# A transformer block on one core: transposes of the identity where the plan leaves TensorE without a product

## The chip, the core and the metric

The kernel runs on one core of one Trainium2 chip. The metric is the device time of one execution in microseconds (us). The core's engines each follow their own list of instructions: TensorE (PE in the profile, its weight loads PEld), VectorE (DVE), ScalarE (ACT), GpSimd (POOL) and SyncE (SP), which issues most transfers. They meet only through semaphores that an instruction waits for or raises.

## The reference

The block takes one sequence of 2048 tokens of width 512. A conditioning vector gives six rows (shift, scale and gate, twice). First comes attention with 32 heads of width 16 on a modulated layer norm, then a "spatial shift" MLP block on another modulated layer norm:

```python
h = _layernorm(x) * (1 + ca) + sa
x = x + ga * _A_ref(h, A_wqkv, A_wo)            # softmax(q k / 4) v, then @ wo
h = _layernorm(x) * (1 + cb) + sb
x = x + gb * _B_ref(h, B_w1, B_w2, B_w3, B_w4)

def _B_ref(x, w1, w2, w3, w4):
    h = _gelu(_layernorm(x) @ w1)                # 512 -> 512
    # four quarters of the columns shifted by +1, -1, +2, -2 tokens
    x1 = x + concat(shifted quarters) @ w2
    return x1 + _gelu(_layernorm(x1) @ w3) @ w4  # 512 -> 1792 -> 512
```

All inputs and the output are float32.

## The kernel before

The 2048 tokens are cut into four chunks (`ci` 0 to 3) of four tiles of 128 tokens. Up to about 1490 us the kernel makes q, k and v and runs attention; then come the **tails**, one per chunk: `tail(ci)` (L1322) and `rest(ci)` (L1622). A tail transposes the attention output (tiles `xT<-ident,osb`), multiplies by wo (`wo`), adds to x, normalises twice (tiles `xf` or `xn`), transposes the result (`xT<-ident,xf` or `xT<-ident,xn`, L1283), and multiplies by w1, w2, w3 and w4 (all named `w` in the profile; `w<-A,wr` are w1 and w3, `w<-wr,g` are w2 and w4). Each product is made of three matmuls per step (`mm3`, lines L377, L379, L381), since every operand stands as a high and a low part. Chunk 0's tail is added while attention still runs; the tails of chunks 1 to 3 are added after it.

The order on each engine is fixed when the program is built. A small planner (`Sched`, from L103) keeps a planned time for each engine (`T["P"]` for TensorE) and a list of generators, each of which yields either planned nanoseconds of a product just issued or a condition that it waits for. `one()` runs the first generator that can go on. Work on ScalarE, VectorE and GpSimd is put in chains and issued by planned time. After attention the loop `while sch.busy(): sch.step()` (L1805) runs everything that is left. `step` (L304) moves TensorE's planned time on by 100 ns:

```python
        t = self.T["P"] + q                      # q = 100.0
        for e in "ADG":
            self.misc(e, max(t, self.T[e]) + 500)
        while self.T["P"] < t and self.one():
            pass
        self.T["P"] = max(self.T["P"], t)
```

Where `one()` finds no generator that can go on, planned time just passes. TensorE's list then has no mark of it; on the chip TensorE goes straight to its next matmul and waits there if its operands aren't ready.

A product's result goes to one of eight PSUM banks. `room()` (L285) says whether the plan has a free one, `dbank` takes it (`take`, L264, the first of `avail`), and the chain that reads it gives it back (`free`). The identity `ident` is a 128x128 float32 tile made at the start; a transpose is a matmul whose other operand it is.

Of the kernel before, what the change touches and what calls it, by code (L numbers as in the profile page):

```python
# [21 lines left out]
P = 128  # L22
# [92 lines left out]
class Sched:  # L115
# [4 lines left out]
    def __init__(self):  # L120
        self.pend = []
        self.chains = []
        self.gens = []
        self.credit = 0.0
        self.T = {"P": 0.0, "A": 0.0, "D": 0.0, "G": 0.0, "S": 1000.0}
        self.end = 0.0
        self.busyG = 0.0, 0.0
        self.gapmin = GAPMIN
        self.banks(8)
# [174 lines left out]
    def step(self, q=100.0):  # L304

        t = self.T["P"] + q
        for e in "ADG":
            self.misc(e, max(t, self.T[e]) + 500)
        while self.T["P"] < t and self.one():
            pass  # L310
        self.T["P"] = max(self.T["P"], t)


# [26 lines left out]
def kernel(ctx, tc, A_x, A_wqkv, A_wo, B_w1, B_w2, B_w3, B_w4, c, w_mod, out):  # L340
    nc = tc.nc
    te, act, dve, pool, dma = nc.tensor, nc.scalar, nc.vector, nc.gpsimd, nc.sync
# [62 lines left out]
    ident = con.tile([P, P], F32, name="ident")  # L405
# [33 lines left out]
    sch = Sched()  # L439
# [3 lines left out]
    def dbank(n):  # L443
        return sch.take(lambda i: psd["d"].tile([P, CH], F32, name=n, tag=f"s{i}" if psd["s"] else f"d{i}", bufs=1))
# [313 lines left out]
    for i in range(NV):  # L758
        t = qp.tile([P, H // 4, 192], BF16, name=f"vt{i}")
# [943 lines left out]
    for k, blk in enumerate(blocks + [[]] * (LAG + CPER)):  # L1703
# [19 lines left out]
        t, start = CIN, 0.0  # L1723
# [68 lines left out]
    with ExitStack() as ex:  # L1792
        ep = ex.enter_context(tc.tile_pool(name="ep", bufs=1, space=PSUM))
        psd["d"], psd["s"] = ep, False
        att.close()
        akx.close()
        tpx = ExitStack()
        tp = tpx.enter_context(tc.tile_pool(name="tp", bufs=1))
        big["A"] = tp.tile([P, 4 * KT * 2 * P], F32R, name="A")
        big["g2"] = tp.tile([P, 4 * KT * 2 * P], F32R, name="g2")  # L1800
        done.add("C")
        rings["f"] = Ring(FRONT * (NC - NB), [("wf", BF)] * BF)
        for ci in range(NB, NC):
            sch.add(tail(ci))
        while sch.busy():  # L1805
            sch.step()
        tpx.close()
# [29 lines left out]
```

## Time and profile before

| | |
|---|---|
| median of 3 runs | 1982.68 us (1981.67 to 1983.91) |
| the profiled execution's own time | 1985.08 us |
| its span, first to last instruction | 1983.3 us |
| TensorE busy | 1935.0 us (98%) |
| VectorE, ScalarE, GpSimd busy | 1535.5, 1497.2, 1546.2 us |
| mean granted TensorE clock | 0.991 |

"Span" is the time that the profile covers; the execution's own time is 1.8 us longer. A busy TensorE isn't one at its peak: matmuls overlap, so the time between two starts in a dense row is less than the time that each is shown with. The granted clock is the share of the full clock that TensorE was given in a stretch; in this trace it is either 1.00 or 0.50 at any moment, so a value between is a mixture. In the timeline a row has the start, the time, the engine, the line, what is written from what, and, in brackets, the idle time ahead of it and the instruction that ended it.

### The profile page before, as it was taken

How to read it: one execution, taken by the hardware profiler on the slowest of the kernel's cores; microseconds unless marked ns; L12 is line 12 of the kernel's file. 1: busy time of each engine (PE TensorE's matmuls, PEld its weight loads, DVE VectorE, ACT ScalarE, POOL GpSimd, SP SyncE). 2: the span in 40 equal slices, each digit the busy share in tenths (PEclk: the TensorE clock that was granted, in tenths of full speed). 3: DMA queues.
4: the chain of work that ended last, by engine and by line, in shares of the span. 5: the costliest groups of instructions: out<-in, count | busy, mean ns of one | idle time of the engine just before them, and what ended most of it. 6: DMA issues, size and time to landing. Idle time of an engine off the chain costs nothing.

```text
span 1983.3 us, 41283 instructions
## 1 busy us (share of the span) xinstructions
PE 1935.0 (98%) x14456; PEld 1158.8 (58%) x14456; DVE 1535.5 (77%) x2672; ACT 1497.2 (75%) x3067; POOL 1546.2 (78%) x1445
## 2 busy tenths in 40 slices
PE   8999999999999999999999999999998999999999
PEld 5745544555444444444444444444456889899998
DVE  6398788888899999999999999999975583423211
ACT  6448898777899999999999999999986454334222
POOL 6359998888899999999999999999995564335222
PEclk9999999999999999999999999999999899999999
DMA  8877656544535353435353535354513587554541
GB/s 303 234 218 182 158 139 169 146 125 126 128 73 109 74 109 74 105 77 108 74 106 77 101 81 106 77 143 124 108 50 144 211 297 283 201 196 152 202 149 69
DMA packets 185502, 277.95 MB, mean 140 GB/s; under 512 B 117104, under 2 KB 127856, under 8 KB 169008
## 3 DMA queue, kind: packets, MB, share of 16 engines
q1 hardware_dynamic: 181792, 267.20, 49.5%
q10 hardware_dynamic: 2304, 4.20, 0.7%
q0 software_dynamic: 1200, 3.93, 0.5%
q8 instruction: 114, 1.87, 0.4%
q14 instruction: 92, 0.75, 0.1%
HBM read 211.81 MB, written 62.91 MB: 139 GB/s over the span
## 4 chain that ended last, share of the span: by engine, by line
PE 77%; DVE 12%; ACT 6%; issue 2%; POOL 1%; DMA 1%; SPq 0%; ACTq 0%; DVEq 0%; POOLq 0%
PE mb L1021 17%; PE sc L1048 11%; PE pv L1122 11%; DVE mx L1017 10%; PE w L379 7%; PE w L381 7%; PE w L377 7%; PE pv L1119 5%; ACT pt L1044 3%; PE ot L1149 3%; PE xT L1283 1%; PE q L379 1%; PE q L377 1%; PE q L381 1%; PE v L377 1%
## 5 line engine op out<-in xcount | busy, mean ns | idle before, releaser
L1017 DVE TENSOR_REDUCE mx<-mb 128x1 f32<-128x512 f32 x2048 | 1251.9, 681 | 56.0 <-PE mb L1021 48.4
L1097 POOL TENSOR_SCALAR pt<-pt 128x1024 f16<-128x1024 uint16 x770 | 1015.2, 1368 | 62.7 <-ACT pt L1044 62.4
L1044 ACT ACTIVATE pt<-sc 128x512 int32<-128x512 f32 x1688 | 891.0, 621 | 89.1 <-PE mb L1021 61.1
L1021 PE MATMUL mb<-kst,qtl 62*128 62x512 f32 x2048 | 784.8, 462 | 18.0 <-ACT pt L1044 9.1
L1048 PE MATMUL sc<-qtl,kst 64*128 64x512 f32 x2048 | 745.2, 451 | 0.5 <-ACT pt L1044 0.4
L1021 PEld LDWEIGHTS mb<-kst,qtl 62*128 62x128 f32 x2048 | 360.3, 192 | 259.6 <-ACT pt L1044 131.9
L1048 PEld LDWEIGHTS sc<-qtl,kst 64*128 64x128 f32 x2048 | 337.8, 185 | 186.5 <-DVE mx L1017 114.9
L1122 PE MATMUL pv<-pt,vst 128*32 128x512 f16 x3376 | 319.0, 396 | 3.3 <-ACT ac L1139 3.3
L1536 POOL TENSOR_TENSOR g<-sq,g 128x256 fp32r<-128x256 f32 (+1 forms) x122 | 95.7, 786 | 179.8 <-ACT g L1535 168.1
L1097 POOL TENSOR_SCALAR xbs<-xbs 128x1024 f16<-128x1024 uint16 x163 | 216.9, 1362 | 3.8 <-ACT xbs L1044 3.7
L1044 ACT ACTIVATE xbs<-sc 128x512 int32<-128x512 f32 x360 | 199.5, 639 | 11.2 <-PE mb L1021 10.1
L1122 PEld LDWEIGHTS <-vst 128*32 128x32 bf16 x4096 | 91.2, 94 | 181.0 <-issue 163.5
L1533 ACT ACTIVATE sq<-w 128x256 f32<-128x256 f32 (+1 forms) x128 | 52.0, 406 | 183.2 <-PE w L381 182.8
L1655 DVE TENSOR_TENSOR x<-x,w 128x512 f32<-128x512 f32 x73 | 49.7, 684 | 168.8 <-PE w L381 168.7
L1119 PE MATMUL pv<-pt,vst 128*32 128x512 f16 (+1 forms) x1688 | 172.8, 392 | 2.8 <-POOL pt L1097 2.8
L379 PE MATMUL w<-A,wr 128*128 128x256 f32 (+1 forms) x520 | 154.3, 297 | 0.6 <-DVE A L360 0.6
L377 PE MATMUL w<-A,wr 128*128 128x256 f32 (+1 forms) x520 | 154.8, 298 | 0.0
L381 PE MATMUL w<-A,wr 128*128 128x256 f32 (+1 forms) x520 | 153.8, 296 | 0.0
L377 PE MATMUL w<-wr,g 128*128 128x512 f32 x270 | 107.0, 397 | 0.0
L381 PE MATMUL w<-wr,g 128*128 128x512 f32 x270 | 106.9, 396 | 0.0
L379 PE MATMUL w<-wr,g 128*128 128x512 f32 x270 | 106.8, 396 | 0.0
L165 ACT ACTIVATE pt<-pt 128x1024 f16<-128x1024 uint16 x74 | 103.1, 1393 | 0.0
(199 smaller groups left out, 2308.1 us busy)
## 6 DMA issues: line engine op xcount, KB each, us to landing
wr<-Ws SPq DMA_DIRECT2D x66, 1024.0 KB, 5.8
vst<-Vs SPq DMA_DIRECT2D x64, 768.0 KB, 5.1
kst<-Ks SPq DMA_DIRECT2D x126, 384.0 KB, 6.2
Ws<-wr SPq DMA_DIRECT2D x14, 1024.0 KB, 5.2
qtl<-Qs SPq DMA_DIRECT2D x128, 96.0 KB, 4.3
Vs<-vt SPq DMA_DIRECT2D x32, 384.0 KB, 4.4
Ks<-qk SPq DMA_DIRECT2D x16, 512.0 KB, 3.9
Qs<-qk SPq DMA_DIRECT2D x16, 512.0 KB, 3.2
```

Of the source, the lines that this page charges most:

```text
L165: fn()
L377: te.matmul(o, lh, rh, start=first, stop=False)
L379: te.matmul(o, lh, rl, start=False, stop=False)
L381: te.matmul(o, ll, rh, start=False, stop=last)
L1017: end = sch.crit("D", 605, e + PX, lambda: dve.reduce_max(mxs[u][:, j, g, c:c + 1], b, axis=AX.X))
L1021: return ready, lambda: te.matmul(b, lhs, kst[u % 3][r, c * CH:(c + 1) * CH], start=True, stop=True), after
L1044: ea = sch.crit("A", 480, e + PX, lambda: act.activation(pt[s][:, j], b, AF.Exp))
L1048: return ready, lambda: te.matmul(b, kst[u % 3][r, kt * P:(kt + 1) * P], qst[u][r], start=True, stop=True), after
L1097: e_low[s] = XP["G"] + sch.crit("G", 1345, ready, lambda: pool.tensor_scalar(o, i, 0.5, 1.0, op0=OP.mult, op1=OP.mult))
L1119: te.matmul(acc[r:r + n, :], v[:, kt + i, c:c + n].bitcast(F16), pt[s + i].bitcast(F16)[:, j, 0::2], start=False, stop=kt == NKT - 2, skip ...
L1122: te.matmul(acc[r:r + 32, :], v[:, kt, r:r + 32], pt[s].bitcast(F16)[:, j, 1::2], start=kt == 0, stop=False, skip_group_check=True)
L1536: ("G", cG(n), lambda: pool.tensor_tensor(lo, sq, hi, op=OP.subtract)), (None, 0, end), bank=b)
```

## The change

`Sched` gets a hook, `idle`, that `step` calls where planned time would pass on TensorE with nothing to issue. After attention the hook is set to `warm()`: if the plan has a free bank and a generator is left, it takes that bank, issues one transpose of the identity into it, and puts the bank back at the head of the free list, so that the next product or the next `warm` takes the same bank. No time is booked for the transpose, and nothing reads the bank afterwards.

```diff
@@ Sched.__init__
         self.end = 0.0
+        self.idle = None
@@ Sched.step
         while self.T["P"] < t and self.one():
             pass
+        if self.T["P"] < t and self.idle:
+            self.idle()
         self.T["P"] = max(self.T["P"], t)
@@ tile_adaln_mha_s2mlp_kernel, after attention
         done.add("C")
+
+        def warm():
+            if sch.room() and sch.gens:
+                b = dbank("warm")
+                te.transpose(b[:, 0:P], ident, ident)
+                sch.open = None
+                sch.avail.insert(0, sch.owner.pop(id(b.tensor)))
+        sch.idle = warm
```

The instructions of VectorE, ScalarE, GpSimd and SyncE, their order and the semaphores that they wait for are the same before and after. TensorE's list gets 99 transposes in five places, rows of 12, 14, 8, 25 and 40, and is otherwise in the same order. The lines of the changed kernel stand 3 further down in this part (L377 is L380, L1283 is L1286).

The first place is between a wo product and a product with w1, both of the tails behind attention. TensorE before, with what each matmul waits for:

```order
L379 MATMUL wo<-wr,A 128x512
L381 MATMUL wo<-wr,A 128x512
L377 MATMUL w_24707<-A,wr 128x256 [waits Activation_49]
L379 MATMUL w_24707<-A,wr 128x256 [waits DVE_49]
L381 MATMUL w_24707<-A,wr 128x256
```

and now:

```order
L384 MATMUL wo<-wr,A 128x512
L1809 MATMUL warm<-ident 128x128 [waits Activation_49]
L1809 MATMUL warm<-ident 128x128 [waits PE_49] x11
L380 MATMUL w_24731<-A,wr 128x256 [waits PE_49,Activation_49]
L382 MATMUL w_24731<-A,wr 128x256 [waits DVE_49]
```

Twelve transposes stand ahead of the product. `PE_49` is the semaphore that TensorE itself raises when a matmul has ended; in the built program each transpose after the first waits for the count that the one just before it raises, and the product waits for the last.

The second and third places are on both sides of the transposes `xT` of `xf`, which wait for VectorE. Before:

```order
L381 MATMUL w_24771<-A,wr 128x256
L1283 MATMUL xT<-ident,xf 128x128 [waits DVE_49] x2
L1283 MATMUL xT<-ident,xf 128x128 x2
L1283 MATMUL xT<-ident,xf 128x128 [waits PE_49]
L1283 MATMUL xT<-ident,xf 128x128 x3
L377 MATMUL w_24819<-wr,g_24471 128x512 [waits DMAHW1_49,PE_49]
```

and now:

```order
L1809 MATMUL warm<-ident 128x128
L1809 MATMUL warm<-ident 128x128 [waits PE_49] x13
L1286 MATMUL xT<-ident,xf 128x128 [waits DVE_49,PE_49]
L1286 MATMUL xT<-ident,xf 128x128 [waits DVE_49]
L1286 MATMUL xT<-ident,xf 128x128 x6
L1809 MATMUL warm<-ident 128x128
L1809 MATMUL warm<-ident 128x128 [waits PE_49] x7
L380 MATMUL w_24887<-wr,g_24471 128x512 [waits DMAHW1_49,PE_49]
```

Fourteen stand ahead of the wait for VectorE, and eight behind the transposes that had that wait, ahead of a product with w2.

The fourth and fifth places are on both sides of the transposes `xT` of `xn`. Before (two rows that repeat the two ahead of them are left out):

```order
L381 MATMUL wo<-wr,A 128x512
L1283 MATMUL xT<-ident,xn 128x128 [waits DVE_49] x3
L1283 MATMUL xT<-ident,xn 128x128 x3
L1283 MATMUL xT<-ident,xn 128x128 [waits PE_49]
L1283 MATMUL xT<-ident,xn 128x128 x2
L377 MATMUL w_24971<-A,wr 128x384 [waits Activation_49]
```

and now:

```order
L1809 MATMUL warm<-ident 128x128 [waits PE_49] x24
L1286 MATMUL xT<-ident,xn 128x128 [waits DVE_49,PE_49]
L1286 MATMUL xT<-ident,xn 128x128 [waits DVE_49] x2
L1286 MATMUL xT<-ident,xn 128x128 x9
L1809 MATMUL warm<-ident 128x128
L1809 MATMUL warm<-ident 128x128 [waits PE_49] x39
L380 MATMUL w_25169<-A,wr 128x384 [waits PE_49,Activation_49]
```

Twenty-five stand ahead of the wait for the third `xn`, and forty behind the transposes, ahead of the product with w3 that reads them.

## The prediction

> **What bounds the kernel now.** I read the page's busy times and chain first, then TensorE by windows from 1500 us on, then the five places in the timeline.
>
> ```profile
> PE 1935.0 (98%) x14456; PEld 1158.8 (58%) x14456; DVE 1535.5 (77%) x2672; ACT 1497.2 (75%) x3067; POOL 1546.2 (78%) x1445
> PE 77%; DVE 12%; ACT 6%; issue 2%; POOL 1%; DMA 1%; SPq 0%; ACTq 0%; DVEq 0%; POOLq 0%
> 1500.00:1550.00 50.00, 42.83 (x255) 0.95 0.55 198
> 1550.00:1600.00 50.00, 49.44 (x275) 0.92 0.66 240
> 1600.00:1650.00 50.00, 47.40 (x242) 0.97 0.83 299
> 1650.00:1700.00 50.00, 50.00 (x319) 1.00 0.59 227
> ```
>
> A window row gives the stretch, its length, TensorE's busy time (matmuls), the granted clock, and DMA. TensorE is the bound: from 1550 us on it has almost no hole, and at 1650 none at a clock of 1.00. So what is put into its list among the tails moves the end by as much, unless it fills a hole or saves clock. There is something to save: the first three rows have holes and a clock under 1. The rows that carry this, cut at the moments at which the clock changes (every 3.41 us, or a multiple of it):
>
> ```profile
> 131.66:135.07 3.41, 2.64 (x15) 1.00 0.96 283
> 135.07:138.48 3.41, 3.41 (x20) 0.50 1.07 397
> 1507.23:1510.64 3.41, 1.58 (x14) 1.00 0.97 329
> 1510.64:1514.05 3.41, 3.41 (x17) 0.50 0.98 406
> 1514.05:1517.46 3.41, 3.41 (x28) 1.00 1.03 378
> 1531.12:1534.53 3.41, 1.83 (x16) 1.00 0.62 259
> 1534.53:1537.94 3.41, 3.41 (x18) 1.00 0.41 115
> 1544.78:1548.19 3.41, 1.66 (x8) 1.00 0.61 199
> 1548.19:1551.60 3.41, 1.80 (x9) 0.50 0.99 344
> 1551.60:1555.02 3.42, 2.86 (x10) 0.50 0.98 321
> 1555.02:1558.43 3.41, 3.41 (x17) 0.50 1.03 411
> 1558.43:1561.84 3.41, 3.41 (x32) 1.00 0.65 264
> 1606.22:1609.63 3.41, 1.36 (x10) 1.00 0.74 279
> 1609.63:1613.04 3.41, 3.41 (x10) 0.50 0.71 259
> ```
>
> A window that TensorE fills badly is followed by one at half clock, and half clock lasts until a window was full. Busy time alone doesn't decide: 1.83 us kept the clock, 2.64 us at 131.66 lost it. What does is how long columns stream, which the starts in dense rows give.
>
> The five places, with the matmuls around them:
>
> ```profile
> 1510.58 3.63 PE L1283 MATMUL xT<-ident,osb 128*128 128x128 f32 x16 [1.83 <-DVE sq L1527]
> 1525.78 0.40 PE L381 MATMUL wo<-wr,A 128*128 128x512 f32 x1
> 1526.01 0.28 PE L377 MATMUL w<-A,wr 128*128 128x256 f32 x1
> 1531.96 0.27 PE L1283 MATMUL xT<-ident,xf 128*128 128x128 f32 x1
> 1533.82 0.98 PE L1283 MATMUL xT<-ident,xf 128*128 128x128 f32 x7 [1.58 <-DVE xf L1427]
> 1534.56 0.48 PE L377 MATMUL w<-wr,g 128*128 128x512 f32 x1
> 1545.84 0.27 PE L1283 MATMUL xT<-ident,xn 128*128 128x128 f32 x1
> 1546.47 0.33 PE L1283 MATMUL xT<-ident,xn 128*128 128x128 f32 x1 [0.36 <-DVE xn L1427]
> 1549.13 0.62 DVE L1427 TENSOR_SCALAR xn<-xbs,tmv,trs 128x512 f32<-128x512 f32 x1
> 1549.80 2.40 PE L1283 MATMUL xT<-ident,xn 128*128 128x128 f32 x10 [3.00 <-DVE xn L1427]
> 1551.85 0.67 PE L377 MATMUL w<-A,wr 128*128 128x384 f32 x1
> 1553.08 0.69 PE L379 MATMUL w<-A,wr 128*128 128x384 f32 x1 [0.56 <-DVE A L360]
> 1553.57 0.52 PE L381 MATMUL w<-A,wr 128*128 128x384 f32 x1
> 1605.40 0.27 PE L1283 MATMUL xT<-ident,xf 128*128 128x128 f32 x1
> 1608.27 0.98 PE L1283 MATMUL xT<-ident,xf 128*128 128x128 f32 x7 [2.60 <-DVE xf L1427]
> ```
>
> The plan and the chip disagree on where the holes are. The row of 12 goes to 1526.01 and the row of 8 to 1534.56, where TensorE has no hole. The 14 go to a hole of 1.58 us, the 25 to one of 0.36 and 3.00, the 40 to one of 0.56. The hole of 2.60 us at 1605 gets none. Together 5.5 us of holes, against 99 transposes.
>
> **What one added transpose costs.** In the program each waits until the one ahead of it has ended, so they don't overlap. No row of before has such a pair, so I bound it. Below: the dense spacing, seven in 0.98 us with the last one 0.33 at most, (0.98 - 0.33)/6 = 0.11 us, if the wait were free. The nearest row is the lone transpose at 1546.47, which waited for another engine and lasted 0.33. To that comes the time from a raised semaphore to the start: VectorE's `xn` ends at 1549.13 + 0.62 = 1549.75, the transpose starts at 1549.80, so 0.05. I take 0.38 us at full clock. At half clock the slowest such transpose tells:
>
> ```profile
> L1283 PE MATMUL xT<-ident,xn x80: 270/273/476, 1496.1 to 1875.7; 128*128 128x128 f32 x80
> ```
>
> Its longest, 0.476, is that at 1549.80; with 0.05 it makes 0.53 us, the upper end. If the semaphore took 0.05 longer, 99 of them would add 5 us.
>
> **Does a row of them hold the clock?** At full clock one streams for 0.11 us of its 0.38, 29%. In the window from 1544.78 wo streams until 1545.84 and two transposes add 0.22: 1.28 of 3.41 us, 38%, and the clock was lost; from 1606.22 TensorE runs only from 1608.27, 40%, lost. From 1531.12 it streams until 1531.96 and then eight transposes, 0.84 + 0.88 = 1.72, 50%, kept. So 29% loses it. At half clock a transpose streams (2.40 - 0.48)/9 = 0.21 us of 0.53, 40%; the window from 1551.60, which was busy for 2.86 us, did not get the clock back, those with 3.41 did. So a row of them also keeps the clock down.
>
> The Trainium skill ("TensorE: Matmul & The Clock Gate", Part 4: PE-mode transpose) says that transposes do not count as TensorE activity for the clock gate. The trace disagrees: the window from 1510.64 held nothing but the 16 transposes of the first row above, and the next ran at 1.00. By the page all 99 would cost 0.53, 4.5 us above my sum, inside the range.
>
> **The sum**, against the profiled execution:
> - The transposes. A row that begins at full clock keeps it until a window ends that is mostly the row, about a window, 3.8 us or 10 transposes. The 12, the 14 and the 25 begin so: 30 at 0.38 = 11.4. The other 69 (2, 4, all 8 and 40, and 15) at 0.53 = 36.6. Together 48.0.
> - The holes that they fill: 1.58 + 0.36 + 3.00 + 0.56 = -5.5. They are filled wholly: 14 last 5.3 us or more, 25 last 9.5, 40 last 15.
> - Real matmuls at half clock. The windows from 1534.53 and 1609.63 are full of the same `w` shape and hold 18 and 10 starts: half clock does 10/18 of the work and loses 0.45 of its time. Before, from 1548.19 to 1558.43: ten transposes, 10 x (0.21 - 0.11) = 1.0, and 5.3 us of `w` from 1553.08 on, 5.3 x 0.45 = 2.4: 3.4 us that may go. After: behind the 8 and behind the 40 the dense product needs the rest of a window and a full one, on average 1.5 x 3.41 = 5.1 us, 2.3 lost each time; behind the 12 half of that, 1.1; 20 transposes 2.0. Together 7.7, so +4.3.
> - The hole at 1605 and the half clock behind it: 2.60 + 0.45 x 3.41 = 4.1 us, which could go if VectorE and GpSimd come there ahead of TensorE, since they stand less in the way of each other while TensorE is late. Between 0 and 4.1 I take 1.5, nearer to nothing, because their lists and the order in them stay.
>
> 48.0 - 5.5 + 4.3 - 1.5 = +45.3 us. What is behind hides none of it:
>
> ```profile
> 1613.04:1950.00 336.96, 336.96 (x2055) 1.00 0.55 204
> 1950.00:1983.30 33.30, 29.62 (x148) 0.98 0.11 40
> ```
>
> TensorE has no hole from 1613 until 1950, and the 3.7 us of holes behind that are the end's own latency, which moves along. 1985.08 + 45.3 = 2030.4; the median lies 2.4 below the profiled execution, so the forecast is **2028 us**.
>
> The other engines get no instruction and no new wait. Queued behind each row are TensorE's next products; ScalarE, VectorE and GpSimd wait for those, and are late with TensorE.
>
> **Rivals.**
> - *The clock holds.* If the gate counts a waiting TensorE as active, or needs an empty window, all 99 cost 0.38 and the 3.4 us come back: 37.6 - 5.5 - 3.4 = +28.7, and with up to 4.1 at 1605, 2007 to 2011 us. For it: a row leaves no gap over 0.3 us. Against: 1.66 and 2.64 us of busy time lost the clock. The Trainium skill ("TensorE: Matmul & The Clock Gate", Part 1) has this rule, that half clock follows an idle window of about 3.4 us; here a gap of 1.83 us (1508.75 to 1510.58) was enough, so the trace does not bear it out.
> - *The waits are free.* If TensorE meets its own semaphore without a stop, 99 x 0.11 = 10.9, less 5.5 and 3.4, +2.0, 1984.7 us. Against it: a semaphore is raised only when a matmul has ended, 0.27 us or more after its start.
> - *Faster than before.* One mechanism: the rows bridge the holes at 1532 and 1546, the clock never falls, and the other engines, ahead by then, close the hole at 1605. It gives 5.5 + 3.4 + 4.1 = 13.0 us, so it decides below 13.0/99 = 0.131 us for a transpose. At the dense spacing it would give 1980.6. That also wants no wait, and the 20 at places without a hole bring nothing.
> - *Dearer.* All at 0.53, and 0.05 more for the semaphore: 57.4 - 5.5 + 4.3 = +56, 2039 us.
>
> **Numbers.** The forecast gets 0.63, the clock holds 0.24, waits free 0.06, faster 0.02, dearer 0.05. The range runs from the clock that holds with the hole at 1605 gone, 2006, to 2038, a microsecond under the dearer end. A measurement here tells about 0.2% (4 us) from no change. Slower by more: 0.92; within it, the free waits and half of the faster case: 0.06; faster: 0.02.
>
> **What would show it.** Five rows of `warm` at 1526, 1535, 1540 and so on, with starts 0.38 us apart at clock 1.00 and 0.53 at 0.50; 0.11 would bring down the first step. Windows of 0.50 inside the rows of 25 and 40 and just behind them show the second; a clock of 1.00 there brings the first rival. The idle time of `xT` before `xf` and `xn` there falls to nothing. The last product should start some 45 us later; if only the hole at 1605 differs from this, its term was mis-sized.

## The result and the profile after

The changed kernel takes 2029.85 us (2028.17 to 2030.13, 4 runs) against 1982.91 us of the kernel before: a ratio of 1.0227, 95% interval 1.0215 to 1.024. By the medians it is 46.9 us slower, by the ratio 45.0. Its profiled execution took 2028.17 us, with a span of 2026.4. In the experiments below, differences in us are the ratio's: the ratio less 1, times the time of the kernel before. Two executions far out of line are in no ratio, one of 4066.31 us (with the row of 40 alone) and one of 2377.72 us (with the bank at the end of the list).

The page of the changed kernel, its busy times and the head of its chain of waits:

```profile
PE 1976.7 (98%) x14555; PEld 1177.7 (58%) x14555; DVE 1534.2 (76%) x2672; ACT 1497.3 (74%) x3067; POOL 1545.5 (76%) x1445
PE 78%; DVE 12%; ACT 5%; issue 2%; POOL 1%; DMA 1%; SPq 0%; ACTq 0%; DVEq 0%; POOLq 0%
```

Only TensorE has more to do: 99 instructions and 41.7 us more. It is as full as before. By stretches (length, TensorE busy, granted clock, DMA):

```profile
1500.00:1550.00 50.00, 46.07 (x228) 0.83 0.45 165
1550.00:1600.00 50.00, 46.06 (x137) 0.67 0.30 109
1600.00:1650.00 50.00, 48.80 (x283) 0.99 0.49 181
```

From 1550 to 1600 TensorE starts 137 matmuls where before it started 275, and the clock is 0.67 where it was 0.92. The timeline of TensorE shows the five rows (start, time, and how many), with the transposes between them:

```profile
1508.84 3.50 PE L1286 MATMUL xT<-ident,osb 128*128 128x128 f32 x16 [1.83 <-DVE sq L1530]
1524.54 4.52 PE L1809 MATMUL warm<-ident 128*128 128x128 f32 x12
1536.53 6.03 PE L1809 MATMUL warm<-ident 128*128 128x128 f32 x14
1542.62 1.97 PE L1286 MATMUL xT<-ident,xf 128*128 128x128 f32 x8
1544.38 4.15 PE L1809 MATMUL warm<-ident 128*128 128x128 f32 x8
1562.07 11.30 PE L1809 MATMUL warm<-ident 128*128 128x128 f32 x25
1573.43 2.82 PE L1286 MATMUL xT<-ident,xn 128*128 128x128 f32 x12
1576.04 19.97 PE L1809 MATMUL warm<-ident 128*128 128x128 f32 x40
1651.37 0.87 PE L1286 MATMUL xT<-ident,xf 128*128 128x128 f32 x6 [2.57 <-DVE xf L1430]
```

The rows take 4.52 + 6.03 + 4.15 + 11.30 + 19.97 = 46.0 us. The transposes of `xf` and `xn` that waited for VectorE before now start with no idle time, but the later `xf` at 1651 waits 2.57 us as it did (2.60). From the first row above to the end of the span it is 2026.4 - 1508.84 = 517.6 us; before, from the same instruction at 1510.58, 472.7. So 44.8 us come from the tails, and the rest of the difference of the medians is scatter ahead of them and between executions.

The same trace by tile, with the shortest, middle and longest duration in ns, and who waited for it:

```profile
L1809 PE MATMUL warm<-ident x99: 270/474/476, 1524.5 to 1595.5; 128*128 128x128 f32 x99
  PEld warm L1809: 29.4, 94
```

Of the 99, 94 were waited for by the next one's weight load, 29.4 us in all. Taken instruction by instruction, the starts stand 0.387 us apart at full clock and 0.533 at half; 42 transposes went at the first, 54 at the second, and three across a change of the clock. Three windows inside the row of 40 show what it did to the clock:

```profile
1577.33:1580.74 3.41, 2.88 (x10) 1.00 0.00 0
1580.74:1584.15 3.41, 3.05 (x7) 0.50 0.00 0
1584.15:1587.57 3.42, 3.00 (x8) 0.50 0.00 0
```

TensorE counts as busy for 2.88 of 3.41 us and still loses the clock, which stays at 0.50 until 1601.2, through the rest of the row and the first 5 us of the product behind it.

### The profile page after: what moved, and what is told of

It reads as the page before. It is cut to its first block, busy times and chain, and to the rows that moved or that the text cites. A ratio compares the mean times of both kernels' runs of the same rounds, so it can differ in the third digit from the quotient of the medians.

```text
span 2026.4 us, 41484 instructions
## 1 busy us (share of the span) xinstructions
PE 1976.7 (98%) x14555; PEld 1177.7 (58%) x14555; DVE 1534.2 (76%) x2672; ACT 1497.3 (74%) x3067; POOL 1545.5 (76%) x1445
## 4 chain that ended last, share of the span: by engine, by line
PE 78%; DVE 12%; ACT 5%; issue 2%; POOL 1%; DMA 1%; SPq 0%; ACTq 0%; DVEq 0%; POOLq 0%
PE mb L1024 17%; PE sc L1051 11%; PE pv L1125 11%; DVE mx L1020 10%; PE w L380 7%; PE w L382 7%; PE w L384 7%; PE pv L1122 5%; PE ot L1152 3%; ACT pt L1047 3%; PE warm L1809 2%; PE xT L1286 1%; PE v L380 1%; PE q L380 1%; PE q L382 1%
## 5 line engine op out<-in xcount | busy, mean ns | idle before, releaser
L380 PE MATMUL w<-A,wr 128*128 128x256 f32 (+1 forms) x520 | 155.5, 299 | 0.3 <-PE warm L1809 0.2
L380 PE MATMUL w<-wr,g 128*128 128x512 f32 x270 | 107.8, 400 | 0.1
```

Of the source, the lines that this page charges most:

```text
L380: te.matmul(o, lh, rh, start=first, stop=False)
```

## The experiments

My theory: an added transpose is dear because it waits until the one ahead has ended, and a row of them loses the clock because columns stream for too small a share of the time. The rivals are that the instructions or the lateness cost the time whatever they wait for, and that transposes as such don't count for the clock.

**One tile for each row.** All 99 transposes stay in their places; only the first of a row takes a bank, and the others write to the same tile, which needs no wait.

```diff
-                b = dbank("warm")
-                te.transpose(b[:, 0:P], ident, ident)
-                sch.open = None
-                sch.avail.insert(0, sch.owner.pop(id(b.tensor)))
+                if w[0] in (0, 12, 26, 34, 59):
+                    w[1] = dbank("warm")
+                    sch.open = None
+                    sch.avail.insert(0, sch.owner.pop(id(w[1].tensor)))
+                te.transpose(w[1][:, 0:P], ident, ident)
+                w[0] += 1
```

> The change with all 99 transposes in their five places, but each row of them goes to one tile, so that only the first of a row can wait and the others stand behind each other without a wait. My theory (the wait for the one ahead is the price, 0.387 us at full clock and 0.533 at half): the spacing falls to 0.11 us, a row streams all the time and holds the clock at 1.00, the 99 cost 10.9 us and fill part of the holes: 1984 to 1987 us, some 44 us less than the change. Rival, what costs is that TensorE is late and others with it, or 99 more instructions as such: it stays above 2015 us. Rival, transposes do not count for the clock gate: spacing 0.21 us at clock 0.50 in the rows of 25 and 40, 1993 to 1997 us.

Measured: 1987.79 us against 1985.63 of the kernel before in the same session, ratio 1.0009 (1.0000 to 1.0018), just above the 1984 to 1987 us that I had written. Its rows in the timeline, and the stretches:

```profile
1525.93 1.47 PE L1814 MATMUL warm<-ident 128*128 128x128 f32 x12
1533.38 1.69 PE L1814 MATMUL warm<-ident 128*128 128x128 f32 x14
1536.06 1.04 PE L1814 MATMUL warm<-ident 128*128 128x128 f32 x8
1548.48 2.89 PE L1814 MATMUL warm<-ident 128*128 128x128 f32 x25
1552.45 1.31 PE L1286 MATMUL xT<-ident,xn 128*128 128x128 f32 x10 [0.58 <-DVE xn L1430]
1553.60 4.53 PE L1814 MATMUL warm<-ident 128*128 128x128 f32 x40
```

```profile
1500.00:1550.00 50.00, 47.67 (x300) 0.97 0.50 177
1550.00:1600.00 50.00, 49.21 (x318) 1.00 0.65 245
1600.00:1650.00 50.00, 47.42 (x249) 1.00 0.81 288
```

The same 99 transposes in the same places now take a quarter of the time (the 40 take 4.53 us and not 19.97) and the clock stays at 1.00 from the first of them on. Nearly all of the change's cost is the wait, with the half clock that comes of it. The first rival falls, and so does the one on transposes, since the rows of 25 and 40 hold nothing else and run at full clock.

**The bank at the end of the list.** One word of the change differs: the next transpose takes another bank, so that it waits for one some places back or for a bank's last reader.

```diff
-                sch.avail.insert(0, sch.owner.pop(id(b.tensor)))
+                sch.avail.append(sch.owner.pop(id(b.tensor)))
```

> The change with one word of it changed: the bank goes back to the end of the free list in place of its head, so that the next transpose takes another bank and waits only for one several places back, or for the last reader of that bank. My theory: a wait for a matmul three or more places back is met already (3 x 0.109 + 0.06 against 0.387) or nearly so, spacing 0.11 to 0.14 us, the clock stays at 1.00; some transposes now wait for VectorE or ScalarE to have read a bank, a few us in all: 1984 to 1994 us. Rival, each transpose costs its 0.387 whatever it waits for: it stays above 2015 us.

Measured: 1986.39 us against 1984.63, ratio 1.0004 (0.9994 to 1.0014), no difference from the kernel before. Two rows of the timeline:

```profile
1547.58 2.89 PE L1809 MATMUL warm<-ident 128*128 128x128 f32 x25
1552.69 4.53 PE L1809 MATMUL warm<-ident 128*128 128x128 f32 x40
```

The spacing is 0.109 us although the program still has a wait ahead of most of them: a wait for a matmul several places back is met by then. So what decides is the distance to what is waited for, and the line that makes it 1 is the one that puts the bank at the head of the list. The few waits for readers of banks that I had expected to cost some microseconds were met too.

**Pairs and fours.** The transposes go to one tile in twos and in fours; each group waits for the one ahead.

```diff
-                if w[0] in (0, 12, 26, 34, 59):
+                if any(w[0] >= s and (w[0] - s) % 2 == 0 and w[0] < e   # % 4 for fours
+                       for s, e in ((0, 12), (12, 26), (26, 34), (34, 59), (59, 99))):
```

> The change with its 99 transposes in pairs: two go to one tile, the next pair waits for the pair ahead. A pair takes 0.387 + 0.109 = 0.496 us at full clock and 0.533 + 0.213 = 0.746 at half, and streams for 0.213 of the 0.496, 43%. My theory (the share of time in which columns stream decides the clock; lost at 40% and below, kept at 50%, so this lies in the open part between): if the clock holds, spacing alternates 0.109 and 0.387, and the rows take about 25 us: +13 to +17 us over before. If it falls, 33 to 37 us: +25 to +30 us. Rival, a TensorE that has an instruction waiting counts as active: no stretch of half clock in any of these kernels, which the change already speaks against. Either way the spacing itself has to be the sum of one full latency and one dense step.

> The same in fours. Four take 0.387 + 3 x 0.109 = 0.714 us and stream for 0.43 of it, 60%, above the 50% that kept the clock before. My theory: the clock stays at 1.00 in all five rows, which take 17 to 18 us; less the holes, +7 to +10 us over before. Rival, any wait inside a row costs the clock: the rows of 25 and 40 fall to half, 28 us and more, +18 us or more.

Measured: pairs 1999.14 us against 1984.63, ratio 1.0067 (1.0052 to 1.0082), +13.3 us (10 to 16 by the interval); fours 1993.04, ratio 1.0036 (1.0022 to 1.0049), +7.1 us (4 to 10). The row of 40 in pairs, and the same row in fours:

```profile
1561.61 9.82 PE L1814 MATMUL warm<-ident 128*128 128x128 f32 x40
1556.48 7.03 PE L1814 MATMUL warm<-ident 128*128 128x128 f32 x40
```

Two windows inside the row of 40 of the pairs:

```profile
1562.61:1566.02 3.41, 3.00 (x14) 1.00 1.02 406
1566.02:1569.43 3.41, 3.06 (x14) 1.00 0.75 310
```

TensorE's busy time is nearly that of the changed kernel's row (2.88 there), with 14 starts in place of 10, and the clock stays. By the starts, 10 transposes of 0.109 us stream in 32% of a window or less and lose the clock; 14 stream in about 45% and keep it. The other rows of the pairs and all rows of the fours run at 1.00 as well. So the busy time of a row of waiting instructions says nothing of its clock. A pair takes 0.496 us and a four 0.714, as I had summed them, but the starts divide this otherwise: in a pair the second starts 0.165 us after the first and the next pair 0.331 after that, not 0.109 and 0.387. The first of a pair, like a lone transpose, waits with its weight load as well and lasts 0.328; the second has its weights loaded while the first runs, and lasts 0.273.

**Which rows cost what.** The change with only its rows of 14 and 25, and with only its row of 40 (calls of `warm` outside these return at once).

```diff
             if sch.room() and sch.gens:
+                w[0] += 1
+                if not any(s < w[0] <= e for s, e in ((12, 26), (34, 59))):   # ((59, 99),) for the 40
+                    return
                 b = dbank("warm")
```

> The change with only its rows of 14 and 25 (those ahead of a wait for VectorE), each transpose still waiting for the one ahead. My theory: 14 cost about 5.9 us and fill 1.58, 25 cost about 11 and fill 3.36; the half clock behind the 25 is about that of before: +12 us, 1993 to 1998 us. Rival, rows ahead of a real wait cost nothing since TensorE would have stood there anyway: 1980 to 1984 us.

> The change with only its row of 40 ahead of the product with w3. My theory: the hole of 3.4 us ahead of it has taken the clock to half already, as before, so nearly all 40 cost 0.533 and fill 0.56 us, and the clock comes back only behind them: 21.3 - 0.6 and about the same loss on real products as before: +19 to +21 us, 2002 to 2004 us. Rival, the row warms the clock for the product (it comes back inside the row, after a window or two): 30 of the 40 at 0.387, and no loss on the product: +14 us or less, under 1998 us.

Measured, against 1985.63: only 14 and 25 1996.02, ratio 1.0049 (1.0034 to 1.0064), +9.7 us (7 to 13 by the interval); only 40 2005.13, ratio 1.0091 (1.0076 to 1.0107), +18.1 us (15 to 21). Both differences agree with the theory and with neither rival; the time of 2005.13 us is a microsecond above the range that I had written, and the kernel before was some 3 us slower here than when it was first measured. The row of 40 alone, in the timeline with the transposes ahead of it:

```profile
1549.09 1.67 PE L1286 MATMUL xT<-ident,xn 128*128 128x128 f32 x10 [3.00 <-DVE xn L1430]
1550.55 21.22 PE L1814 MATMUL warm<-ident 128*128 128x128 f32 x40
```

and three of its windows, inside the row and behind it:

```profile
1560.14:1563.55 3.41, 3.06 (x7) 0.50 0.01 5
1573.79:1577.20 3.41, 3.41 (x17) 0.50 0.00 0
1577.20:1580.61 3.41, 3.41 (x31) 1.00 0.02 5
```

It starts at half clock, never leaves it in 21.2 us, and the clock comes back only after a window full of real products. A row put there to keep TensorE warm held it cold. The rows ahead of a real wait aren't free either, as the timeline of the kernel with 14 and 25 shows:

```profile
1531.48 5.30 PE L1814 MATMUL warm<-ident 128*128 128x128 f32 x14
1550.55 11.90 PE L1814 MATMUL warm<-ident 128*128 128x128 f32 x25
```

They last 17.2 us where the holes were 1.58 and 0.36 + 3.00.

**Transposes without waits, where the holes are.** From the kernel before: 14, 3 + 27 and 23 transposes of the identity ahead of the transposes of `xf`, `xn` and the later `xf` that wait, written to the place which the next transpose overwrites.

```diff
+    BRIDGE = {49: 14, 57: 3, 58: 27, 93: 23}
+    nth = [0]
@@ transposed
                 for i in range(nt):
+                    for _ in range(BRIDGE.get(nth[0], 0)):
+                        te.transpose(b3[:, j, i * P:(i + 1) * P], ident, ident)
+                    nth[0] += 1
                     te.transpose(b3[:, j, i * P:(i + 1) * P], src(k, i), ident)
```

> The kernel before with 67 transposes of the identity without waits between them, put where the trace of before has its holes and nowhere else: 14 ahead of the second transpose of xf (hole 1.58 us), 3 and 27 ahead of the second and third of xn (0.36 and 3.00 us), 23 ahead of the second of the later xf (2.60 us). They write to the place that the next transpose then overwrites. My theory: the holes stay as long but are filled, the half clock from 1548 to 1558 (3.4 us lost) and that from 1609 to 1613 (1.5 us lost) go: 1977 to 1979 us, 4 to 6 us faster than before. Rival, transposes do not count for the clock gate: both stretches of half clock stay, 1982 to 1984 us, the same as before.

Measured: 1983.81 us against 1985.63, ratio 0.9988 (0.9979 to 0.9997): faster, by 2.4 us (0.6 to 4.2 by the interval; 1.8 by the medians), half of the 4 to 6 us that I expected, and the only version here that beats the kernel before. The clock, and what TensorE now waits for:

```profile
1550.00:1600.00 50.00, 47.33 (x287) 1.00 0.69 251
1600.00:1650.00 50.00, 49.68 (x270) 1.00 0.82 300
```

```profile
1551.79 1.31 PE L1289 MATMUL xT<-ident,xn 128*128 128x128 f32 x10
1555.07 0.44 PE L379 MATMUL w<-A,wr 128*128 128x384 f32 x1 [1.79 <-DVE A L360]
1556.76 0.44 PE L379 MATMUL w<-A,wr 128*128 128x384 f32 x1 [0.38 <-DVE A L360]
```

Both stretches of half clock are gone, as the theory has it. But the ten transposes end a microsecond sooner after their start, and the product behind them waits for VectorE to split what they made: 1.79 + 0.38 us where before it was 0.56. In these two traces the slow clock had been hiding a wait, and 1.6 us of the gain went into it. The clock gave less, too, than these two traces promise. In that of the kernel before, the two stretches of half clock take 0.5 x (10.24 + 3.41) / 1983.3 = 0.0034 off the mean clock; over all executions here the mean clock rose by only 0.0015, from 0.9934 (21 of the kernel before) to 0.9949 (11 with the bridges). Either an ordinary execution of the kernel before loses less than the one that I had worked from, or the new wait of 1.79 us costs the clock in some executions; which, and how the missing half of the gain divides, is not shown.

## Why the prediction was right

The time came out at 2029.85 against 2028 forecast, by the mechanism that was forecast; two of its terms were off, by 2.0 and 1.5 us, and that they nearly cancel is luck.

- *The price of one transpose* was right: 0.387 and 0.533 us measured for 0.38 and 0.53. The bound from below, 0.11, is what it costs without the wait, as the row in one tile shows.
- *The row loses the clock* was right, by the streaming time and not by the busy time: windows with 2.88 us of busy time lost it. The pairs put the border between 32% and 45%, which agrees with the 38% and 40% (lost) and the 50% (kept) that I had read from the trace before. This also settles the rival of a clock that holds.
- *How many at which clock*: 42 and 54, and three between, where I had put 30 and 69. A row keeps the full clock somewhat longer, and the row of 40 got it back for one window. The window ahead of that one was not quite full, as I had thought it must be: TensorE was busy for 3.29 us of it, with the end of the twelve `xn` transposes and the first of the 40. The rows took 46.0 us, not 48.0.

```profile
1573.92:1577.33 3.41, 3.29 (x14) 0.50 0.82 337
```

- *The holes filled*, 5.5 us, came out as forecast: none of the first waits for `xf` and `xn` is left.
- *Real matmuls at half clock*, +4.3: what remains of the 44.8 us is 44.8 - 46.0 + 5.5 = 4.3. It agrees, but as a remainder. Counted from the trace by the prediction's own rates it is nearly the same: half clock lies on 3.4 us of products behind the 12 (1529.55 to 1532.96), 4.8 behind the 8 (1548.60 to 1553.44), 5.1 behind the 40 (1596.17 to 1601.22) and on twenty transposes, 13.3 x 0.45 + 20 x 0.10 = 8.0, less the 3.4 of before: +4.6.
- *The hole at 1605* was the term that was mis-sized: -1.5 forecast, 0 measured. The wait is there with 2.57 us and the half clock behind it too. From 1608.27 to 1651.37 it moved by 43.1 us, as the span did (2026.4 - 1983.3). The chain that ends in that wait runs alike in both traces: it leaves TensorE at transposes at 1582.63 before and 1625.75 now, and reaches VectorE's `xf` at 1606.82 and 1649.92, 43.1 us later each. What ScalarE, GpSimd and VectorE do there hangs on TensorE's results, so being late together didn't let them get ahead.
- *From the profiled execution to the median* I took off 2.4 us; here the profiled execution lies 1.7 below its median. That step has no more worth than the scatter of single executions.

The Trainium skill's sentence that transposes don't count for the clock gate ("TensorE: Matmul & The Clock Gate", Part 4: PE-mode transpose) isn't borne out: the rows without waits consist of nothing else and stay at 1.00. The window from 1510.64 in the trace before, by which I had doubted it, showed this less cleanly than I wrote: a product began in it at 1513.89.

## What to carry to other kernels

Before filler work is put on an engine, look at what each piece waits for: the same 99 transposes cost 44.8 us when each waits for the one just ahead and some 2 us or less (intervals up to 3.6) when it doesn't. A row of instructions that wait for each other looks busy in the profile and can still lose the clock; count the time in which columns stream. And take the places of holes from the trace, not from the plan: the plan put 60 of the 99 where the chip had 0.56 us of holes.

## What the runs showed of the hardware that I had not expected

- In a chain of dependent transposes the starts stand 0.387 us apart at full clock. In pairs the first of the next pair starts 0.331 us after the second of the one ahead, whose weights were loaded early, but that second starts 0.165 us after its first: early weight loading moved the time and saved none.
- A wait on TensorE's own semaphore for a matmul several places back costs nothing that can be seen: spacing 0.109 us with the wait (bank at the end of the list) and without (one tile for each row).
- The hole at the later `xf` (2.60 us) cost the clock in the kernel before, and the same hole (2.58 us) didn't with one tile for each row, where it fell across two windows with 2.12 us of TensorE time in each:

```profile
1606.43:1609.84 3.41, 2.12 (x13) 1.00 0.76 264
1609.84:1613.26 3.42, 2.12 (x13) 1.00 0.53 196
1613.26:1616.67 3.41, 3.41 (x18) 1.00 0.96 344
```

The hole is 2.57 to 2.60 us long in eight of the traces here. Half clock follows it in five (before, after, 14 and 25 alone, 40 alone, pairs) and not in three (one tile, fours, bank at the end of the list). Where a window begins differs from one trace to the next, so a hole of this size costs its half clock, 1.5 us, in some executions and not in others. That may be a part of the scatter between executions of one kernel (1981.51 to 1988.82 us in 21 runs of the kernel before); it was not measured on executions of one kernel.
